# Top-k attention and two MLPs on one core: a planner writes the order of all five engines, and the first MLP's gate moves from VectorE to ScalarE and GpSimd

## The chip, the cores and the metric

One core of a Trainium2 chip runs the whole program. The metric is the device time of one execution in microseconds (us). A core has five engines, each with a queue of its own that it works through in order: TensorE (PE in the profile; its weight loads are shown as PEld), VectorE (DVE), ScalarE (ACT), GpSimd (POOL) and SyncE (SP), which here only issues DMAs.

## The reference

Everything is computed in float32 accuracy; the weights come as float64.

```
scores = q @ k.T / 8          # batch 4, heads 8, 576 x 576, head size 64
kth    = the 32nd largest score of each row
attn   = softmax of the scores >= kth, 0 elsewhere
x      = (attn @ v), heads side by side: 2304 x 512
h      = x @ w_in             # 512 x 2048
g      = h where h >= 1; 0 where h <= -1; (h + 1)^2 / 4 between
y      = g @ w_out            # 2048 x 512
h2     = max(y @ w_in2, 0)
out    = (h2 * h2) @ w_out2   # 2304 x 512
```

## The kernel before

**Tiles.** The 2304 tokens are 18 row tiles T of 128 rows. In attention a row tile has 8 slots, one for a head (two half heads where a tile straddles two batches), 144 slots in all. For each slot TensorE makes the scores (`scores`, L497 and L498), ScalarE copies them to SBUF (`scores_copy`, L502), and VectorE finds the 32 largest: four MAX8 (L514) with three MATCH_REPLACE8 between them (L516). ScalarE takes the exponential (`exp`, L528), with a bias that GpSimd makes (`exp_bias`, L523); VectorE multiplies it by the mask (`mask`, L532). ScalarE and GpSimd split the result into two float16 parts (`prob_hi` L544, `prob_lo` L548 and L549), a DMA transposes them (L554), and 14 matmuls multiply them with v (`attend`, L569) into one of 7 places of a PSUM bank, `acc`. The buffers `W` of the search and the exponential are a ring of three. `x_part` divides four slots by their sums and, after the second four, splits x and transposes it by DMA (L592) into `T_x`.

**The MLPs.** Each matrix is split into two float16 parts, so a product is three matmuls. A group n is a quarter of one layer of one row tile: 12 matmuls into a PSUM bank `h` (`mlp_in`, L710 to L712; two banks), the gate, the split of its result into `g`, a transpose by DMA to `gT` (`mlp_trans`, L746), and 12 matmuls into `o` (`mlp_out`, L757 to L759). There are 144 groups: 72 of the first MLP (m = 1) and 72 of the second (m = 2). They go in fours: four of the first MLP for tile T, then four of the second for tile T - 1. Between the two MLPs `y_finish` scales, splits and transposes y.

**The gate before.** With scaled constants, the first MLP's gate is min(square(relu(A1 h + B1)), relu(A2 h - G) + G). `mlp_act` makes the square in the buffer `r` (L721, L722) and the second relu in place of h in PSUM (L723), all on ScalarE; `mlp_gate` adds G and takes the minimum on VectorE (L733). `mlp_split` then takes a buffer `g` (a ring of two, `gbufs`), copies r into its first half as float16 on ScalarE (L740) and the remainder into its second half on GpSimd (L741). The second MLP's gate is a relu and a square on ScalarE (L725, L726).

**The weights** are loaded from float64 (64 chunks of 512 KB), put together by ScalarE, GpSimd and VectorE (`w_decode`, L181 to L183), measured by small matmuls (`w_norm`, L196), scaled and split (`w_scale`, `w_split`), all within the first 300 us or so.

**The order.** A plan by hand, `PLAN`, gives each piece of work a step; a slot is 8 steps. `at(u, fn, ...)` puts a call at step u, `chain` a list of calls at offsets from one, and `run_steps` calls them step by step; `early_fns` does the same for the search. The group with index n is at step 8 (12 + n), so a tile's first MLP comes some 12 slots after the slots of its index. VectorE and SP run in just the order of these calls (`MANUAL`, from step -6 on). The order of TensorE, ScalarE and GpSimd from there on is made by the framework, which simulates a timeline of the program while it is built.

Of the kernel before, what the change touches and what calls it, by code (L numbers as in the profile page):

```python
# [7 lines left out]
F16 = mybir.dt.float16  # L8
F32 = mybir.dt.float32
I32 = mybir.dt.int32  # L10
U16 = mybir.dt.uint16
BF16 = mybir.dt.bfloat16
AF = mybir.ActivationFunctionType
ALU = mybir.AluOpType
AX = mybir.AxisListType

P = 128
# [15 lines left out]


PLAN = dict(
    kch=(0, 0, 0, 1), vch=(0, 0, 1), scale=(0, 1, 2, 3, 4, 5), dch=(0, 1, 3), qch=(0, 0, 3, 4), k0=(-5, -4, -2),
    d0=(-8, -6, -4, -2), l0=(-9, -6), n0=(0, 1, 0, 1, 2, 3), q01=-5, v0l=-2, v0n=(5, 7, 9, 11), v0s=14, vn=60, vnd=7,
    vnl=18, vs=241, meet=248, mc1=252, m2c0=121, m2c1=265, v0=(21, 25, 29, 33, 37, 41, 45, 49), kv1=(254, 10, 289, 6),
# [13 lines left out]
    dsa_i2=(0, 2, 4, 6, 8, 10, 12, 14), dsa_o2=(0, 2, 4, 6, 8, 10, 12, 14), u0=-6,  # L52
    prio=(3, 0, 0, 2, 2, 3, 4, 5, 5, 6, 1, 7), gbufs=2, g_tr=18,
)
MANUAL = {mybir.EngineType.DVE, mybir.EngineType.SP}


@with_exitstack
def tile_topk_attention_mlp_mlp(
# [9 lines left out]
    out: bass.AP,  # L69
):  # L70
    nc = tc.nc
    PE, ACT, DVE, POOL, SP = nc.tensor, nc.scalar, nc.vector, nc.gpsimd, nc.sync

    cpool = ctx.enter_context(tc.tile_pool(name="cpool", bufs=1))
    pool = ctx.enter_context(tc.tile_pool(name="pool", bufs=2))
    small = ctx.enter_context(tc.tile_pool(name="small", bufs=2))
    ps_s = ctx.enter_context(tc.tile_pool(name="ps_s", bufs=1, space=bass.MemoryType.PSUM))
    ps_a = ctx.enter_context(tc.tile_pool(name="ps_a", bufs=1, space=bass.MemoryType.PSUM))
    ps_j = ctx.enter_context(tc.tile_pool(name="ps_j", bufs=1, space=bass.MemoryType.PSUM))
    ps_h = ctx.enter_context(tc.tile_pool(name="ps_h", bufs=2, space=bass.MemoryType.PSUM))  # L80
    ps_o = ctx.enter_context(tc.tile_pool(name="ps_o", bufs=2, space=bass.MemoryType.PSUM))

    def ctile(name, n=1):
        return cpool.tile([P, n], F32, tag=name, name=name)
# [130 lines left out]
    def w_split(name, c):  # L215
# [3 lines left out]
        if name in DIAG_AT:  # L219
# [106 lines left out]
    def k_prep(b, i):  # L326
        hl = lambda: ld["khl", b, i]

        on_dve = 4 * b + i in PLAN["dk"]

# [30 lines left out]
    def v_prep(b, h):  # L361
        on_dve = 8 * b + h in PLAN["dv"]

        def scale():
            t = ld["v", b, h]
            if not on_dve:
                POOL.tensor_scalar(t, t, sv[:, b : b + 1], 1.0, op0=ALU.mult, op1=ALU.mult)
            vs = pool.tile([P, 2, 5, D1], F16, tag="vst", name=f"vst_{b}_{h}", bufs=PLAN["vbufs"])
            POOL.memset(vs[:, 0, :, D : D + 1], 1.0)
            POOL.memset(vs[:, 1, :, D : D + 1], 0.0)  # L370
            vst[b, h] = vs

# [12 lines left out]

        return [scale, split_hi, split_lo]
# [4 lines left out]
    def tile_parts(T, j):  # L391

        if T in (4, 13):
            b = (0 if T == 4 else 2) + j // 4
            s0 = 512 if j < 4 else 0
            jj = j % 4
            return [(0, 64, b, 2 * jj, s0), (64, 64, b, 2 * jj + 1, s0)]
        if T < 4:
            b, s0 = 0, T * P
        elif T < 9:  # L400
            b, s0 = 1, 64 + (T - 5) * P
        elif T < 13:
# [21 lines left out]
    def q_scale(T):  # L424
# [268 lines left out]
    NGROUP = 8 * NTILE + 4  # L693
# [3 lines left out]
    def group(n):  # L697
        return group_[n]

    hps, gs, ops_, rt = {}, {}, {}, {}  # L700
# [11 lines left out]
        PE.matmul(h, src[:, 1, fb, :], w_hi(w, c, 0, 512), start=False, stop=(fb == 3))  # L712


    def mlp_act(n):
        m, T, j = group(n)
        r = pool.tile([P, 512], F32, tag="r", name=f"r_{n}", bufs=2)
        rt[n] = r
        h = hps[n].rearrange("p a b -> p (a b)")
        if m == 1:  # L720
            ACT.activation(r, h, AF.Relu, bias=B1[:, column(T)], scale=A1[:, column(T)])  # L721
            ACT.activation(r, r, AF.Square)  # L722
            ACT.activation(h, h, AF.Relu, bias=NG[:, column(T)], scale=A2[:, column(T)])  # L723
        else:
            ACT.activation(r, h, AF.Relu, scale=C2)  # L725
            ACT.activation(r, r, AF.Square)  # L726

    def mlp_gate(n):
        m, T, j = group(n)
        r = rt[n]  # L730
        if m == 1:
            h = hps[n].rearrange("p a b -> p (a b)")
            DVE.scalar_tensor_tensor(r, h, G[:, column(T)], r, op0=ALU.add, op1=ALU.min)  # L733
        del hps[n]

    def mlp_split(n):
        m, T, j = group(n)
        r = rt.pop(n)
        g = pool.tile([P, 2, 512], F16, tag="g", name=f"g_{n}", bufs=PLAN["gbufs"])
        ACT.activation(g[:, 0], r, AF.Copy)  # L740
        POOL.tensor_tensor(g[:, 1], r, g[:, 0], op=ALU.subtract)  # L741
        gs[n] = g

    def mlp_trans(n):
        t = pool.tile([P, 2, 4, P], F16, tag="gT", name=f"gT_{n}", bufs=2)
# [60 lines left out]
    ev = {}  # L806
# [9 lines left out]
    def at(u, fn, *args):  # L816
        ev.setdefault(u, []).append((fn, args))

    def chain(u, offsets, make, *args):
        def start():  # L820
            steps = make(*args)
            assert len(steps) == len(offsets), (make, len(steps))
            for o, step in zip(offsets, steps):
                if o:
                    at(u + o, step)
                else:
                    step()

        at(u, start)

    def k_chain(b, i, u):
        if b:
            at(u - PLAN["klead"], k_load, b, i)
# [27 lines left out]
    for c in range(2, 6):  # L861
        chain(PLAN["d0"][c - 2], PLAN["dch"], w_decode, "i1", c)
# [37 lines left out]
    dec = {n: PLAN["dec_" + n].__getitem__ for n in W}  # L900
# [24 lines left out]
    N0 = PLAN["N0"]  # L925
    order = [(1, 0, j) for j in range(4)] + ([(2, 0, j) for j in range(4)] if PLAN["early"] else [None] * 4)
# [49 lines left out]

    def run_steps(u0, u1):
        for u in range(u0, u1):
            fns = ev.pop(u, [])
            pre = [f for f in fns if f[0] in (scores, exp, exp_bias)]  # L980
            for fn, args in pre:
                if fn is not exp_bias:
                    fn(*args)
            early_fns(u)
            for fn, args in pre:
                if fn is exp_bias:
                    fn(*args)

            key = dict(zip((prob_hi, prob_lo, prob_trans, scores_copy, mlp_out, mlp_act, mlp_gate, mlp_split, mlp_trans, attend, attend, mlp_in), PLAN["prio"]))
            for fn, args in sorted((f for f in fns if f not in pre), key=lambda f: key.get(f[0], 9)):  # L990
                fn(*args)
            while u in ev:
                for fn, args in ev.pop(u):
                    fn(*args)

    with tc.manual_schedule():
        run_steps(-9, PLAN["u0"])
    with tc.manual_schedule(engines=MANUAL):
        run_steps(PLAN["u0"], 8 * (N0 + NGROUP + 6))
    assert not ev, sorted(ev)  # L1000


# [28 lines left out]
```

## Time and profile before

| what | value |
|---|---|
| median of 3 runs | 1179.51 us (1178.97 to 1180.36) |
| time of the profiled execution | 1181.12 us |
| its span, first to last instruction | 1179.3 us |
| mean granted TensorE clock | 0.968 of full speed |
| busy: PE, DVE, ACT, POOL | 1007.4, 979.3, 852.9, 685.5 us |
| the same as shares of the span | 85%, 83%, 72%, 58% |
| instructions | 20481 |

The busy time of an engine is the time in which it executes something; of TensorE the ends are modelled and overlap the next start, so the distance between starts tells more. The profile also lists groups of like instructions by line, what an engine waited for (and which engine's work released it), and the instructions in order of time. The profiled execution took 1.6 us more than the median.

### The profile page before, as it was taken

The page shows a single profiled execution, that of the slowest core. Times are in us where ns is not written, and L with a number is a line of the kernel's source. Part 1 is how long each engine was busy: PE and PEld are TensorE (multiplying, and loading weights), DVE is VectorE, ACT ScalarE, POOL GpSimd, SP SyncE. Part 2 cuts the span into 40 slices and gives each one's busy share as a digit, 9 for nine tenths or more (in the row PEclk, how much of TensorE's full clock was granted, in tenths as well). Part 3 has the DMA queues.
Part 4 walks back from the last instruction along what each step waited for, and adds up shares of the span by engine and source line. Part 5 has one row for each costly group of instructions (what it writes and reads, how often), then busy time and mean ns, then how long its engine had stood idle before and what let it go on. Part 6 is the DMA issues. An engine that isn't in the chain of part 4 may idle for free.

```text
span 1179.3 us, 20481 instructions
## 1 busy us (share of the span) xinstructions
PE 1007.4 (85%) x6700; PEld 488.3 (41%) x6700; DVE 979.3 (83%) x2111; ACT 852.9 (72%) x1613; POOL 685.5 (58%) x1004
## 2 busy tenths in 40 slices
PE   2248775568899999999888999999999999999997
PEld 1123332223344444444434444444444444444443
DVE  5798957958998999999888999999899999997100
ACT  5659987687677677878676887878676877867532
POOL 4774548858665745455766665456766555554221
PEclk9999988678899999999999999999999999999999
DMA  9977767665496766866886776767877666756532
GB/s 244 362 202 209 197 175 180 136 121 95 85 183 136 125 121 109 148 132 122 140 148 117 141 121 111 146 124 146 161 134 122 123 124 115 127 99 123 80 60 58
DMA packets 463386, 165.20 MB, mean 140 GB/s; under 512 B 441776, under 2 KB 448944, under 8 KB 463280
## 3 DMA queue, kind: packets, MB, share of 16 engines
q1 hardware_dynamic: 463280, 163.90, 68.6%
q8 instruction: 52, 0.85, 0.3%
q14 instruction: 54, 0.44, 0.1%
HBM read 55.31 MB, written 4.72 MB: 51 GB/s over the span
## 4 chain that ended last, share of the span: by engine, by line
PE 25%; DVE 24%; DMA 19%; ACT 12%; POOL 11%; issue 7%; SPq 2%; POOLq 0%; ACTq 0%; DVEq 0%
DVE W L516 9%; DVE m L514 8%; PE h L710 4%; DMA gT<-g 4%; PE o L757 4%; DVE W L532 4%; PE h L711 4%; PE h L712 4%; PE o L758 3%; PE o L759 3%; DMA T_x<-hl_x 3%; POOL g L741 2%; POOL S L549 2%; DMA qT<-qhl 2%; DMA wall<-in_moe_w_out_dram 2%
## 5 line engine op out<-in xcount | busy, mean ns | idle before, releaser
L514 DVE MAX8 m<-W 128x8 f32<-128x576 f32 x432 | 312.5, 745 | 0.1
L757 PE MATMUL o<-wall,gT 128*128 128x512 f16 x576 | 222.1, 386 | 25.7 <-DMA gT<-g 25.3
L741 POOL TENSOR_TENSOR g<-r,g 128x512 f16<-128x512 f32 x144 | 172.6, 1199 | 108.4 <-ACT g L740 70.0
L758 PE MATMUL o<-wall,gT 128*128 128x512 f16 x576 | 221.4, 384 | 0.0
L759 PE MATMUL o<-wall,gT 128*128 128x512 f16 x576 | 221.2, 384 | 0.0
L516 DVE MATCH_REPLACE8 W<-m,W 128x576 f32<-128x576 f32 x288 | 213.6, 742 | 0.0
L549 POOL TENSOR_TENSOR S<-W,S 128x512 f16<-128x512 f32 x144 | 167.4, 1162 | 0.0
L528 ACT ACTIVATE W<-S,nb,esc 128x576 f32<-128x576 f32 x144 | 124.7, 866 | 15.8 <-DVE m L514 15.0
L532 DVE SCALAR_TENSOR_TENSOR W<-S,m,W 128x576 f32<-128x576 f32 x144 | 134.1, 931 | 1.0 <-ACT W L528 1.0
L548 POOL TENSOR_TENSOR S<-W,S 128x64 f16<-128x64 f32 x144 | 46.9, 326 | 149.6 <-ACT S L544 148.9
L544 ACT ACTIVATE S<-W 128x576 f16<-128x576 f32 x144 | 98.1, 681 | 49.0 <-DVE W L532 48.4
L569 PE MATMUL acc<-vst,pT 128*128 128x65 f16 (+1 forms) x2240 | 106.2, 197 | 28.6 <-DMA pT<-S 26.8
L569 PEld LDWEIGHTS <-pT 128*128 128x128 f16 (+1 forms) x2240 | 94.6, 102 | 81.1 <-DMA pT<-S 36.4
L710 PE MATMUL h<-wall,T_x 128*128 128x512 f16 x288 | 112.0, 389 | 12.4 <-DMA T_x<-hl_x 11.2
L502 ACT ACTIVATE S<-s 128x576 f32<-128x576 f32 x144 | 93.0, 646 | 40.5 <-DMA pT<-S 20.6
L497 PE MATMUL s<-kst,qT 128*128 128x512 f16 (+1 forms) x320 | 99.3, 406 | 26.7 <-ACT S L502 14.6
L710 PE MATMUL h<-wall,T_y 128*128 128x512 f16 x288 | 110.1, 382 | 3.9 <-DVE r L733 3.8
L711 PE MATMUL h<-wall,T_x 128*128 128x512 f16 x288 | 111.4, 387 | 0.0
L712 PE MATMUL h<-wall,T_x 128*128 128x512 f16 x288 | 111.0, 385 | 0.0
L712 PE MATMUL h<-wall,T_y 128*128 128x512 f16 x288 | 110.2, 382 | 0.0
L711 PE MATMUL h<-wall,T_y 128*128 128x512 f16 x288 | 110.1, 382 | 0.0
L514 DVE MAX8 m<-S 128x8 f32<-128x576 f32 x144 | 107.9, 749 | 2.4 <-ACT S L502 2.4
(167 smaller groups left out, 1875.3 us busy)
## 6 DMA issues: line engine op xcount, KB each, us to landing
wall<-in_moe_w_in_dram SPq DMA_DIRECT2D x32, 512.0 KB, 6.1
wall<-in_moe_w_out_dram SPq DMA_DIRECT2D x30, 512.0 KB, 5.1
out_dram<-ob SPq DMA_DIRECT2D x18, 256.0 KB, 2.1
l_q<-in_q_dram SPq DMA_DIRECT2D x16, 256.0 KB, 3.8
n_v<-in_v_dram SPq DMA_DIRECT2D x24, 144.0 KB, 3.0
n_k<-in_k_dram SPq DMA_DIRECT2D x12, 288.0 KB, 3.1
l_k<-in_k_dram SPq DMA_DIRECT2D x12, 288.0 KB, 3.3
pT<-S SPq DMA_TRANSPOSE x144, 3.4
```

What stands on the lines that cost most here:

```text
L514: ops.append(lambda src=src, mi=mi: DVE.max(mi, src))
L516: ops.append(lambda src=src, mi=mi: DVE.match_replace(w, mi, src, -3.0e38))
L532: DVE.scalar_tensor_tensor(d["e"], d["s"], d["m"][:, TOPK - 1 : TOPK], d["e"], op0=ALU.is_ge, op1=ALU.mult,)
L549: POOL.tensor_tensor(pc[:, S + 64 :], p[:, 0:512], pc[:, 0:512], op=ALU.subtract)
L569: PE.matmul(acc[r0 : r0 + rn, t % 7, :], pT[:, pc, r0 : r0 + rn], vs[:, part, c, :], start=(i == 0), stop=(i == len(terms) - 1),)
L710: PE.matmul(h, src[:, 0, fb, :], w_hi(w, c, 0, 512), start=(fb == 0), stop=False)
L711: PE.matmul(h, src[:, 0, fb, :], w_lo(w, c, 0, 512), start=False, stop=False)
L712: PE.matmul(h, src[:, 1, fb, :], w_hi(w, c, 0, 512), start=False, stop=(fb == 3))
L741: POOL.tensor_tensor(g[:, 1], r, g[:, 0], op=ALU.subtract)
L757: PE.matmul(o, g[:, 0, fb, :], w_hi(w, c, 0, 512), start=(c == 0), stop=False)
L758: PE.matmul(o, g[:, 0, fb, :], w_lo(w, c, 0, 512), start=False, stop=False)
L759: PE.matmul(o, g[:, 1, fb, :], w_hi(w, c, 0, 512), start=False, stop=(c == 15))
```

## The change

Three things change. First, every call is now noted in a book instead of being issued; the book lists what each operation reads and writes, prices it, and then plans the five engines together. In the plan an engine that is free takes, among the operations that are ready, the one with the lowest rank, which is its step and then its place in the program. All five engines are then given the order of that plan. An operation may be planned at most 12 MAX8 ahead of its place (`WINDOW`), a load or store no earlier than the MAX8 just before it. Buffers of a ring are given out in the plan as they come free. Second, `soon` subtracts steps from the rank of some work: 8 steps for the scores and their copy, the exponential and its split and transpose, and `attend`; 24 steps for `x_part`. Third, the first MLP's gate becomes min(square(relu(A1 h + B1)) , G) + relu(A2 h - G), where the minimum is taken ahead of the square, with RHO, whose square is G: a new GpSimd tensor_scalar on r, the same ScalarE work (the second relu now goes to SBUF, into the buffer g, which is therefore taken in `mlp_act`), and a GpSimd addition in place of VectorE's instruction.

```diff
+    soon=dict(s=8, att=8, a=8, x=24),
-MANUAL = {mybir.EngineType.DVE, mybir.EngineType.SP}
...
+    def note(self, engine, method, fn, args, kwargs):
...
+        op.load = method == "dma_start"
+        if op.load:
+            if self.beat:
+                deps.add(self.beat[-1])
+        elif len(self.beat) > WINDOW:
+            deps.add(self.beat[-WINDOW])
+        if engine == "DVE" and method == "max":
+            self.beat.append(op.n)
...
+        op.key = (self.step + self.shift, op.n)
...
+    def costs(self, engine, method, args, kwargs, outs, ins):
+        n = outs[0].elements() if outs else 0
+        if engine == "PE":
+            a = args[1].tile.dtype
+            c = max(n * (4 if a is F32 else 1) / 2370.0, 0.044)
+            return c, c + 0.2
+        if engine == "DVE":
+            if method in ("max", "match_replace"):
+                n = 576
+            c = 0.06 + n / 960 + (0.07 if method != "max" else 0)
+            return c, c + 0.09
+        if engine == "ACT":
+            c = 0.17 + n / 1400 + 0.1 * sum(isinstance(kwargs.get(k), View) for k in ("bias", "scale", "accum_out"))
+            return c, c + 0.12
+        if engine == "POOL":
+            c = 0.2 + n / 550 if method == "tensor_tensor" else 0.22 + n / 1100
+            return c, c + 0.06
...
+            t, e = best
+            while soon[e] and soon[e][0][0] <= t:
+                op = ops[heapq.heappop(soon[e])[1]]
+                heapq.heappush(now[e], (op.key, op.n))
+            op = ops[heapq.heappop(now[e])[1]]
+            op.start = t
...
+WINDOW = 12
...
     def mlp_act(n):
         m, T, j = group(n)
         r = pool.tile([P, 512], F32, tag="r", name=f"r_{n}", bufs=2)
         rt[n] = r
-        h = hps[n].rearrange("p a b -> p (a b)")
+        h = hps.pop(n).rearrange("p a b -> p (a b)")
+        gs[n] = g = pool.tile([P, 2, 512], F16, tag="g", name=f"g_{n}", bufs=PLAN["gbufs"])
         if m == 1:
+            u = g.rearrange("p a b -> p (a b)").bitcast(F32)
             ACT.activation(r, h, AF.Relu, bias=B1[:, column(T)], scale=A1[:, column(T)])
-            ACT.activation(r, r, AF.Square)
-            ACT.activation(h, h, AF.Relu, bias=NG[:, column(T)], scale=A2[:, column(T)])
+            ACT.activation(u, h, AF.Relu, bias=NG[:, column(T)], scale=A2[:, column(T)])
+            POOL.tensor_scalar(r, r, RHO[:, column(T)], 0.0, op0=ALU.min, op1=ALU.max)
         else:
             ACT.activation(r, h, AF.Relu, scale=C2)
-            ACT.activation(r, r, AF.Square)
+        ACT.activation(r, r, AF.Square)
 
     def mlp_gate(n):
         m, T, j = group(n)
-        r = rt[n]
         if m == 1:
-            h = hps[n].rearrange("p a b -> p (a b)")
-            DVE.scalar_tensor_tensor(r, h, G[:, column(T)], r, op0=ALU.add, op1=ALU.min)
-        del hps[n]
+            POOL.tensor_tensor(rt[n], rt[n], gs[n].rearrange("p a b -> p (a b)").bitcast(F32), op=ALU.add)
 
     def mlp_split(n):
-        m, T, j = group(n)
-        r = rt.pop(n)
-        g = pool.tile([P, 2, 512], F16, tag="g", name=f"g_{n}", bufs=PLAN["gbufs"])
+        r, g = rt.pop(n), gs[n]
         ACT.activation(g[:, 0], r, AF.Copy)
         POOL.tensor_tensor(g[:, 1], r, g[:, 0], op=ALU.subtract)
-        gs[n] = g
...
+    def urgent(fn, made):
+        soon = SOON.get(KIND.get(fn, ""), 0)
+        if not soon:
+            return made
+
+        def call(*args):
+            book.shift, before = -soon, book.shift
+            made(*args)
+            book.shift = before
+
+        return call
...
-    with tc.manual_schedule():
-        run_steps(-9, PLAN["u0"])
-    with tc.manual_schedule(engines=MANUAL):
-        run_steps(PLAN["u0"], 8 * (N0 + NGROUP + 6))
-    assert not ev, sorted(ev)
+    run_steps(-9, 8 * (N0 + NGROUP + 6))
+    assert not ev, sorted(ev)
     with tc.manual_schedule():
+        book.emit(book.order())
```

## Rows read from the trace of the kernel before

**Rows 1.** Stretches of the span: busy us of each engine, its instructions, clock, DMA share.

```profile
0.00:420.00 420.00, 289.72 (x1933) 140.74 (x1934) 342.67 (x760) 310.27 (x609) 274.71 (x393) 0.92 0.72 174
420.00:1080.00 660.00, 626.41 (x4312) 306.11 (x4311) 625.37 (x1330) 499.71 (x934) 384.17 (x582) 0.99 0.71 129
```

**Rows 2.** The same stretches, line L532 (the mask, one a slot) alone.

```profile
420.00:1080.00 660.00, 91.93 (x99) 0.99 0.71 129
```

**Rows 3.** The same stretches, line L740 (the copy into g, one a group) alone.

```profile
420.00:1080.00 660.00, 60.90 (x98) 0.99 0.71 129
```

**Rows 4.** TensorE in order of time around 960 us: start, duration, instruction.

```profile
959.79 0.38 PE L710 MATMUL h<-wall,T_x 128*128 128x512 f16 x1
...
962.38 0.38 PE L757 MATMUL o<-wall,gT 128*128 128x512 f16 x1
...
965.62 0.38 PE L497 MATMUL s<-kst,qT 128*128 128x512 f16 x1
...
966.11 0.38 PE L569 MATMUL acc<-vst,pT 128*128 128x65 f16 x7
966.33 0.38 PE L757 MATMUL o<-wall,gT 128*128 128x512 f16 x1
```

**Rows 5.** The stretches of rows 1, line L733 (VectorE's gate) alone.

```profile
0.00:420.00 420.00, 11.81 (x16) 0.92 0.72 174
420.00:1080.00 660.00, 37.46 (x51) 0.99 0.71 129
```

**Rows 6.** What VectorE waited for from 0 to 420 us: total, times, longest.

```profile
DVE r L733 <- ACT r L722: 20.6, 3, 11.6
```

**Rows 7.** What VectorE waited for from 420 to 1080 us.

```profile
DVE W L516 <- POOL S L549: 9.3, 11, 2.5
...
DVE r L733 <- ACT r L722: 3.8, 5, 1.4
```

**Rows 8.** Groups of instructions, shapes apart: busy us, mean ns of one, idle before.

```profile
L741 POOL TENSOR_TENSOR g<-r,g 128x512 f16<-128x512 f32 x144 | 172.6, 1199 | 108.4 <-ACT g L740 70.0 <-issue 28.2 <-POOL S L549 2.9
...
L723 ACT ACTIVATE h<-h,NG,A 128x512 f32<-128x512 f32 x72 | 53.4, 741 | 0.0
L733 DVE SCALAR_TENSOR_TENSOR r<-h,G,r 128x512 f32<-128x512 f32 x72 | 53.0, 736 | 44.0 <-ACT r L722 43.5
...
L722 ACT ACTIVATE r<-r 128x512 f32<-128x512 f32 x72 | 45.1, 627 | 0.0
...
L434 POOL TENSOR_SCALAR l_q<-l_q,sq 128x512 f32<-128x512 f32 x18 | 13.6, 756 | 8.9 <-DVE sq L94 8.5
```

**Rows 9.** Line L532: shortest, median and longest duration in ns, first and last start.

```profile
L532 DVE SCALAR_TENSOR_TENSOR W<-S,m,W x144: 799/810/1660, 39.6 to 1084.5; 128x576 f32<-128x576 f32 x144
```

**Rows 10.** All engines in order of time: one group of the first MLP.

```profile
960.64 0.78 ACT L721 ACTIVATE r<-h,B,A 128x512 f32<-128x512 f32 x1 [0.78 <-PE h L712]
...
964.46 0.72 DVE L733 SCALAR_TENSOR_TENSOR r<-h,G,r 128x512 f32<-128x512 f32 x1
...
965.37 0.62 ACT L740 ACTIVATE g<-r 128x512 f16<-128x512 f32 x1
...
966.06 1.16 POOL L741 TENSOR_TENSOR g<-r,g 128x512 f16<-128x512 f32 x1 [0.17 <-ACT g L740]
...
967.50 1.27 SPq L746 DMA_TRANSPOSE gT<-g  x1
```

**Rows 11.** The DMAs into gT: us from issue to landing, shortest, median, longest.

```profile
DMA to landing us min/median/max: 3.0/3.1/5.4
```

**Rows 12.** 30 us with TensorE's clock lowered (columns as in rows 1).

```profile
210.00:240.00 30.00, 14.61 (x104) 7.71 (x104) 29.02 (x65) 22.04 (x49) 24.91 (x34) 0.65 0.58 130
```

**Rows 13.** VectorE in order of time: the last mask.

```profile
1084.47 1.16 DVE L532 SCALAR_TENSOR_TENSOR W<-S,m,W 128x576 f32<-128x576 f32 x1 [0.35 <-ACT W L528]
```

**Rows 14.** ScalarE in order of time: first and last of the 16 copies into g after it.

```profile
1086.91 0.63 ACT L740 ACTIVATE g<-r 128x512 f16<-128x512 f32 x1
...
1167.42 0.63 ACT L740 ACTIVATE g<-r 128x512 f16<-128x512 f32 x1
```

More of the change, by code (lines that the diff above doesn't have):

```diff
@@ L54, with __init__, __getitem__, _by @@
 )
-MANUAL = {mybir.EngineType.DVE, mybir.EngineType.SP}
+class View:
+    __slots__ = ("tile", "ap", "how")
+    def __init__(self, tile, ap, how=()):
+        self.tile, self.ap, self.how = tile, ap, how
+    def __getitem__(self, key):
+        return View(self.tile, self.ap[key], self.how + (("__getitem__", (key,), {}),))
+    def _by(self, name, *args, **kwargs):
+        return View(self.tile, getattr(self.ap, name)(*args, **kwargs), self.how + ((name, args, kwargs),))
+    def rearrange(self, *args, **kwargs):
+        return self._by("rearrange", *args, **kwargs)
+    def bitcast(self, dtype):
+        return self._by("bitcast", dtype)
+    def unsqueeze(self, axis):
+        return self._by("unsqueeze", axis)
+    def to_broadcast(self, shape):
+        return self._by("to_broadcast", shape)
+    def real(self):
+        at = self.tile.room()
+        for name, args, kwargs in self.how:
+            at = getattr(at, name)(*args, **kwargs)
+        return at
+    def cover(self):
+        size = SIZES[self.ap.dtype]
+        (pitch, parts), *free = self.ap.ap
+        p0, at = divmod(self.ap.offset, pitch)
+        free = sorted((s, n) for s, n in free if n > 1 and s)
+        run = 1
+        while free and free[0][0] == run:
+            run *= free.pop(0)[1]
+        last = at + run + sum(s * (n - 1) for s, n in free)
+        step = free[0][0] if len(free) == 1 else 0
+        return p0, p0 + parts, at * size, last * size, step * size, run * size
+    def elements(self):
+        n = 1
+        for _, m in self.ap.ap[1:]:
+            n *= m
+        return n
@@ new lines, with meet, __init__, room @@
+SIZES = {F16: 2, BF16: 2, U16: 2, F32: 4, I32: 4}
+def meet(a, b):
+    if a[1] <= b[0] or b[1] <= a[0] or a[3] <= b[2] or b[3] <= a[2]:
+        return False
+    step = a[4] or b[4]
+    if step and a[4] in (0, step) and b[4] in (0, step):
+        (x, nx), (y, ny) = ((c[2], c[5] if c[4] else c[3] - c[2]) for c in (a, b))
+        if nx < step and ny < step:
+            d = (y - x) % step
+            return d < nx or step - d < ny
+    return True
+class Room:
+    def __init__(self, ring, shape, dtype, name):
+        self.ring, self.shape, self.dtype, self.name = ring, shape, dtype, name
+        self.writes, self.reads, self.first, self.left, self.end, self.at = [], [], None, 0, 0.0, None
+    def room(self):
+        if self.at is None:
+            pool, kwargs = self.ring.pool, self.ring.kwargs
+            self.at = pool.tile(self.shape, self.dtype, name=self.name, **kwargs)
+        return self.at
@@ L58, in tile_topk_attention_mlp_mlp, with _bacc_ @@
+WINDOW = 12
+def _bacc_():
+    import concourse.bacc
+    return concourse.bacc
 @with_exitstack
@@ L71, in tile_topk_attention_mlp_mlp, with rings @@
     nc = tc.nc
[L72 to L81, printed above, removed]
+    book = Book(nc)
+    PE, ACT, DVE, POOL, SP = (
+        book.engine(n, e)
+        for n, e in (("PE", nc.tensor), ("ACT", nc.scalar), ("DVE", nc.vector), ("POOL", nc.gpsimd), ("SP", nc.sync))
+    )
+    def rings(name, bufs, **space):
+        return book.pool(ctx.enter_context(tc.tile_pool(name=name, bufs=bufs, **space)), bufs)
+    psum = dict(space=bass.MemoryType.PSUM)
+    cpool, pool, small = rings("cpool", 1), rings("pool", 2), rings("small", 2)
+    ps_s, ps_a, ps_j, ps_h, ps_o = (
+        rings(n, m, **psum) for n, m in (("ps_s", 1), ("ps_a", 1), ("ps_j", 1), ("ps_h", 2), ("ps_o", 2))
+    )
     def ctile(name, n=1):
@@ L817, in at @@
         ev.setdefault(u, []).append((fn, args))
+    SOON = PLAN["soon"]
+    KIND = {x_part: "x", mlp_in: "in", mlp_act: "act", mlp_gate: "act", mlp_split: "act", mlp_trans: "act", mlp_out: "out",
+            y_finish: "y", o_finish: "y", w_decode: "dec", w_norm: "dec", w_scale: "split", w_split: "split", norm: "n",
+            norm_load: "n", k_prep: "kv", v_prep: "kv", k_load: "kv", v_load: "kv", exp: "a", exp_bias: "a",
+            prob_hi: "a", prob_lo: "a", prob_trans: "a", attend: "att", scores: "s", scores_copy: "s", q_scale: "q", q_prep: "q"}
+    def urgent(fn, made):
[7 more added lines that the diff above has]
+        return call
     def chain(u, offsets, make, *args):
         def start():
-            steps = make(*args)
+            steps = [urgent(make, step) for step in make(*args)]
             assert len(steps) == len(offsets), (make, len(steps))
@@ L978, in run_steps @@
         for u in range(u0, u1):
+            book.step = u
             fns = ev.pop(u, [])
@@ L982, in run_steps @@
                 if fn is not exp_bias:
-                    fn(*args)
+                    urgent(fn, fn)(*args)
             early_fns(u)
@@ L986, in run_steps @@
                 if fn is exp_bias:
-                    fn(*args)
+                    urgent(fn, fn)(*args)
             key = dict(zip((prob_hi, prob_lo, prob_trans, scores_copy, mlp_out, mlp_act, mlp_gate, mlp_split, mlp_trans, attend, attend, mlp_in), PLAN["prio"]))
             for fn, args in sorted((f for f in fns if f not in pre), key=lambda f: key.get(f[0], 9)):
-                fn(*args)
+                urgent(fn, fn)(*args)
             while u in ev:
```

147 lines of the change are left out of this document (added).

## The prediction

> **What bounds the kernel now.** I read the stretches first, because shares of the whole span mix stages [rows 1]. From 420 to 1080 us VectorE is busy 625.4 of 660 us, 95%; TensorE shows 626.4, but its ends are modelled, so I count starts. Twelve matmuls of a group start from 959.79 to 962.38, 0.216 us apart; the four score matmuls take 0.49 us to the next start, seven of a slot's 14 `attend` matmuls 0.22 us [rows 4]. A slot costs TensorE 0.93 us, a group 24 x 0.216 = 5.18 us. The stretch holds 99 masks [rows 2] and 98 groups [rows 3], so TensorE needs 92 + 508 = 600 us of 660, 91%. The two engines run nearly level at one slot and one group per 6.67 us, VectorE ahead. Before 420 us neither is full: VectorE idles 77.3 us, and its longest single cause is the gate, which in the hand-written order waits for ScalarE's square 20.6 us in three places [rows 1, 6]. Behind each of those waits stand the next slot's MAX8 and the weights' decoding. At the end attention is over: the last mask ends at 1085.6 [rows 13], 16 groups still pass their copy into g [rows 14], and 93.7 us of matmuls follow, 5.18 us a group. So the time is VectorE's road to the last mask plus a tail of TensorE's.
>
> **The gate leaves VectorE.** Gone from 420 to 1080 us: 51 instructions, 37.5 us [rows 5], and 3.8 us of waiting for them [rows 7]. VectorE then needs 625.4 - 37.5 = 588 us there. ScalarE keeps its three instructions, so it costs nothing; the second relu writes SBUF instead of PSUM, priced as before at 0.74 us [rows 8]. GpSimd gets a tensor_scalar, nearest row 0.76 us (L434, same shape and type), and an addition, nearest row 1.20 us (L741, but float16 out): 1.96 us for each of 72 groups, 141 us [rows 8]. Their cover is GpSimd's idle time, 660 - 384 = 276 us in the stretch [rows 1], of which 51 x 1.96 = 100 us go: 58% busy becomes 77% of a stretch of 631 us. If that cover fails, VectorE's search is late next: its MATCH_REPLACE8 already waits 9.3 us for GpSimd to be done with an old W [rows 7]. Twice that would be 9 us more.
>
> **The two engines' common port.** The mask takes 0.81 us at the median, 1.66 at most [rows 9], 0.93 in the mean of the stretch [rows 2]: 0.12 us of it is excess, beside a GpSimd 58% busy. At 77% I put it at 0.16, so 99 masks cost 4 us more, and VectorE needs 592 us, still under TensorE's 600: nothing in the sum. The Trainium skill, page "SBUF — State Buffer", section "Who interferes with whom", speaks against the change here: a VectorE instruction with two SBUF inputs and a GpSimd instruction that reads SBUF exclude each other, and the later one is blocked until the other has ended. By that an average mask would lose half a GpSimd instruction times GpSimd's busy share, an estimate of 0.35 us now and 0.46 then, 11 us in the stretch, VectorE would stand level with TensorE, and the sum would be some 5 us later, 1130. The longest mask agrees with a full block, the median doesn't.
>
> **The planned order, 420 to 1080 us.** The floor is TensorE's 600 us. VectorE today fills 95% of its time; I give TensorE the same, 600 / 0.95 = 631, so **-29 us**. Ends: -60 (the floor) and 0 (today's pace stays, the freed time turns into waiting). I take the middle because the two loads, 600 and 592, lie so near each other that each will wait for the other.
>
> **The planned order, 0 to 420 us.** The gate's 20.6 us of waiting vanish, and of its 16 instructions' 11.8 us [rows 5] I count half, since VectorE has idle time to lose there: **-27 us**. Ends: -89 (all 77.3 us of idleness and the 11.8 filled) and +23. The loss end is the clock: TensorE's granted clock means 0.92 in this stretch [rows 1], 0.65 from 210 to 240 us, between its levels of 1.2 and 2.4 GHz, where it was busy 14.6 of 30 us [rows 12]. The planner prices every matmul at the full clock, and 8% of 289.7 us is 23. I stay near the middle, at the one wait that surely goes; weights and their decoding are late next.
>
> **Advance in rank.** x_part and its 18 transposes go ahead by 24 steps, the slots' ScalarE, GpSimd, TensorE and SP work by 8. They move past pT, gT and loads in SP's queue, an issue costing 1.27 us [rows 10], and past g's remainders on GpSimd. An issue moved ahead delays others by its own length and frees it later: 18 x 1.27 = 23 us of queue over the whole span, hidden because SP only issues. I cost it at 0, ends -10 and +23. The search's calls on VectorE don't pass through `urgent`, so their rank is unchanged.
>
> **The tail.** A planned step may be at most 12 MAX8, three slots, ahead, so a backlog of the same kind is left at the last mask. I take 0; ends -11 (16 groups at 5.18 are 83 us, against 93.7) and +5 (four last first-MLP groups whose chain grows by 1.96 - 0.74 = 1.2 us each, without other matmuls to cover it).
>
> **Sum.** 1181.1 (the profiled execution) - 29 - 27 = 1125; its like among the runs, at the median's distance of -1.6, would be 1123.5, and I keep **1125**.
>
> **Rivals.** *Slower: the ring of two g buffers.* A g is now taken at the second relu, not at the copy. Today it is held from 965.37 to the issue at 967.50 plus 3.1 us of transfer [rows 10, 11], 5.2 us. Afterwards: 0.76 + 0.63 + 1.20 + 0.62 + 1.20 on ScalarE and GpSimd and 3.1 of transfer, 7.5 us, plus six hand-overs. In today's group they cost 0.44 us each: 6.86 us from the first relu to the issue, of which 4.65 is work on the path, over five hand-overs [rows 8, 10]. That makes 10.2 us, or 5.1 us a group with two buffers, under the 6.4 us a slot and a group would then take. The ring decides from 12.8 us of holding on, 0.9 us a hand-over, twice today's. For it: in four first-MLP groups in a row GpSimd has 3.9 us a slot plus 1.96, 5.8 of 6.4, 91% busy, so what queues there waits. At 1.3 us a hand-over the hold is 15.3 us, 7.65 a group, 1.25 us too much for each of 72: +90, **1215**. Against it: the plan counts the ring and can put second-MLP groups between. *No gain: an order that is too tight.* The planner prices the mask at 0.06 + 0.60 + 0.07 = 0.73 us, the trace at 0.93 [rows 2]; in a fixed order 0.2 x 99 = 20 us of lateness can reach TensorE each time, and the early part may gain nothing: 1181 - 29 + 20 = 1172, and with GpSimd's W wait doubled, 1181; centre **1176**. *Better: the early stretch fills.* With 60 us instead of 27 early, and 45 instead of 29 later, **1076**. That the change doesn't do what it says is no case here beyond the unadvanced search: the gate's removal doesn't hang on ranks.
>
> **Chances and range.** Forecast (1085 to 1165) 0.60; better (under 1085) 0.06; too tight (1165 to 1190) 0.12, of which 0.05 is a gain, 0.05 no change, 0.02 a loss; the ring (over 1190) 0.22. A difference under 0.2% (2.4 us) can't be told from none here. So faster 0.71, same 0.05, slower 0.24. The range runs from 1085 to 1200: it leaves out the better case and two thirds of the ring's. The forecast's own range is 1085 to 1165.
>
> **What would show it.** Right: the gate's line gone from VectorE, masks per 60 us in the middle up from 9.0 to 9.4, the last mask near 1030, a tail still near 94 us, GpSimd busy near 825 us. The early part is right if VectorE's idle time before 420 us falls by some 20 us or more. Wrong: TensorE waiting for gT or `h` in first-MLP groups while ScalarE's second relu waits for a transpose that has not read g (the ring); a mask whose mean is over 1.1 us (the port); VectorE's MATCH_REPLACE8 waiting for GpSimd's remainder far beyond 20 us in all; TensorE's clock lower for longer than before.

## The result and the profile after

The changed kernel takes **1162.16 us** (median; 1160.56 to 1163.93) beside 1179.24 us for the kernel before: a ratio of 0.9866, with a 95% interval of 0.9847 to 0.9885. It is 1.3% faster, where 4.6% was forecast: 37 us over the forecast of 1125, inside the range of 1085 to 1200. Its profiled execution has a span of 1158.8 us, 20.5 us under the 1179.3 of before, so the two traces can be set against each other (the medians lie 17.1 us apart; the traced execution was the fastest of its four).

All instructions now come out of the book and so bear one line, L339 (L341 where a run's file is two lines longer); one tells them apart by tiles. First the page's busy times after, share of the span and instructions:

```profile
PE 1000.6 (86%) x6700; PEld 483.2 (42%) x6700; DVE 985.1 (85%) x2039; ACT 855.3 (74%) x1613; POOL 833.6 (72%) x1148
```

VectorE has 72 instructions fewer (2039 for 2111), those of the gate, which were 53.0 us of busy time [rows 8], and yet it is busy for 985.1 us where it was 979.3. GpSimd has 144 instructions more and is busy for 833.6 us (forecast: 825). The stretches of the kernel after, with the columns of [rows 1], cut shortly before its last mask:

```profile
0.00:420.00 420.00, 304.80 (x2073) 148.12 (x2074) 375.61 (x794) 329.39 (x644) 329.31 (x446) 0.93 0.77 182
420.00:1050.00 630.00, 594.75 (x4116) 289.12 (x4115) 602.46 (x1229) 477.48 (x890) 463.06 (x659) 1.00 0.69 129
```

In the middle VectorE reads 96% of the stretch (95% before [rows 1]) and holds 95 masks and 95 copies into g in 630 us: 6.63 us for a slot and a group, where it was 6.67. Nothing was gained there. To see where the 20.5 us came from I use the 40th of the 144 masks, well behind the weights, and the last one. In order of time on VectorE, before and then after:

```profile
397.33 1.13 DVE L532 SCALAR_TENSOR_TENSOR W<-S,m,W 128x576 f32<-128x576 f32 x1
```

```profile
363.92 0.81 DVE L339 SCALAR_TENSOR_TENSOR W<-S,m,W 128x576 f32<-128x576 f32 x1
...
1054.18 0.82 DVE L339 SCALAR_TENSOR_TENSOR W<-S,m,W 128x576 f32<-128x576 f32 x1 [0.99 <-ACT W L339]
```

With the last mask of before at 1084.47 [rows 13]: the start of the 40th comes 33.4 us earlier, the 104 slots from there to the last take 690.3 us for 687.1 (**+3.2**), and from the last mask to the end it is 104.6 for 94.8 us (**+9.8**). Together -20.4.

**Where VectorE's 53 us went.** Groups of the kernel after, shapes apart (busy us, mean ns | idle before); all second matmuls of the MLPs (`o`) are one group here:

```profile
L339 PE MATMUL o<-wall,gT 128*128 128x512 f16 x1728 | 425.2, 385 | 45.7 <-DMA gT<-g 42.9 <-POOL wall L339 1.3 <-DVE m L339 1.1
...
L339 DVE MAX8 m<-W 128x8 f32<-128x576 f32 x432 | 322.7, 753 | 5.0
L339 DVE SCALAR_TENSOR_TENSOR W<-S,m,W 128x576 f32<-128x576 f32 x144 | 145.7, 1012 | 4.6 <-ACT W L339 4.5
...
L339 POOL TENSOR_TENSOR r<-r,g 128x512 f32<-128x512 f32 x72 | 93.8, 1302 | 21.5 <-ACT r L339 21.3
...
L339 POOL TENSOR_SCALAR r<-r,RHO 128x512 f32<-128x512 f32 x72 | 51.2, 711 | 20.6 <-ACT r L339 20.3
```

and before, the same MAX8 and the first of the three lines of second matmuls, the only one with waits for gT:

```profile
L757 PE MATMUL o<-wall,gT 128*128 128x512 f16 x576 | 222.1, 386 | 25.7 <-DMA gT<-g 25.3
L514 DVE MAX8 m<-W 128x8 f32<-128x576 f32 x432 | 312.5, 745 | 0.1
```

The mask's mean rose to 1012 ns (931 before, the median of 810 unchanged), 11.6 us in all. More lies between the instructions. VectorE in order of time, first the order by hand, then the planned one:

```profile
453.16 0.74 DVE L516 MATCH_REPLACE8 W<-m,W 128x576 f32<-128x576 f32 x1
453.82 0.75 DVE L514 MAX8 m<-S 128x8 f32<-128x576 f32 x1
```

```profile
920.99 0.74 DVE L339 MATCH_REPLACE8 W<-m,W 128x576 f32<-128x576 f32 x1
921.76 0.76 DVE L339 MAX8 m<-W 128x8 f32<-128x576 f32 x1
923.10 0.76 DVE L339 MAX8 m<-S 128x8 f32<-128x576 f32 x1 [0.57 <-ACT S L339]
923.96 0.09 DVE L339 MATCH_VALUE_LOAD W<-m,S 128x8 f32 x1
```

The order by hand runs two searches in turn: the next instruction belongs to the other slot and starts 0.66 us after the one before, ahead of its end. In the planned order the MAX8 at 921.76 works on what the MATCH_REPLACE8 just before it wrote and starts 0.77 us after it, behind its end; the MATCH_VALUE_LOAD at 923.96 comes 0.86 us after the MAX8 that it needs. Counted over the trace (an instruction of over 0.5 us whose successor starts 20 to 110 ns after its end, not ahead of it) there are 12 such pairs before and 329 after, at 0.12 us and more each some 42 us of VectorE's time. With the masks that is 54 us: about what the gate had used.

### The profile page after: what moved, and what is told of

Same layout as the page of the kernel before. It is cut to its first block, busy times and chain, and to the rows that moved or that the text cites. A ratio compares the mean times of both kernels' runs of the same rounds, so it can differ in the third digit from the quotient of the medians.

```text
span 1158.8 us, 20462 instructions
## 1 busy us (share of the span) xinstructions
PE 1000.6 (86%) x6700; PEld 483.2 (42%) x6700; DVE 985.1 (85%) x2039; ACT 855.3 (74%) x1613; POOL 833.6 (72%) x1148
## 4 chain that ended last, share of the span: by engine, by line
DVE 28%; POOL 24%; PE 18%; DMA 12%; issue 8%; ACT 8%; SPq 1%; POOLq 0%; DVEq 0%; ACTq 0%
DVE W L339 14%; DVE m L339 11%; PE o L339 8%; PE h L339 8%; POOL wall L339 6%; POOL S L339 5%; DMA gT<-g 4%; POOL g L339 4%; POOL r L339 3%; ACT S L339 2%; DMA qT<-qhl 1%; ACT r L339 1%; SPq L339 1%; DMA wall<-in_moe_w_in_dram 1%; PE s L339 1%
## 5 line engine op out<-in xcount | busy, mean ns | idle before, releaser
L339 PE MATMUL o<-wall,gT 128*128 128x512 f16 x1728 | 425.2, 385 | 45.7 <-DMA gT<-g 42.9
L339 DVE MAX8 m<-W 128x8 f32<-128x576 f32 x432 | 322.7, 753 | 5.0
L339 PEld LDWEIGHTS <-gT 128*128 128x128 f16 x1728 | 160.8, 99 | 248.6 <-DMA gT<-g 69.0
L339 POOL TENSOR_TENSOR S<-W,S 128x64 f16<-128x64 f32 (+1 forms) x288 | 213.7, 760 | 69.5 <-ACT S L339 68.6
L339 POOL TENSOR_TENSOR g<-r,g 128x512 f16<-128x512 f32 x144 | 174.3, 1211 | 85.8 <-ACT g L339 65.5
L339 DVE MATCH_REPLACE8 W<-m,W 128x576 f32<-128x576 f32 x288 | 213.5, 741 | 0.0
L339 PE MATMUL h<-wall,T_x 128*128 128x512 f16 x864 | 207.3, 383 | 0.0
L339 PE MATMUL h<-wall,T_y 128*128 128x512 f16 x864 | 205.6, 379 | 1.0 <-ACT r L339 1.0
L339 ACT ACTIVATE W<-S,nb,esc 128x576 f32<-128x576 f32 x144 | 124.3, 863 | 38.8 <-DVE m L339 33.1
L339 DVE SCALAR_TENSOR_TENSOR W<-S,m,W 128x576 f32<-128x576 f32 x144 | 145.7, 1012 | 4.6 <-ACT W L339 4.5
L339 ACT ACTIVATE S<-W 128x576 f16<-128x576 f32 x144 | 98.3, 682 | 58.7 <-DVE W L339 54.6
L339 DVE MAX8 m<-S 128x8 f32<-128x576 f32 x144 | 107.7, 748 | 18.7 <-ACT S L339 18.6
L339 PE MATMUL s<-kst,qT 128*128 128x512 f16 (+3 forms) x640 | 103.9, 298 | 22.0 <-ACT S L339 18.7
L339 PEld LDWEIGHTS <-T_x 128*128 128x128 f16 x864 | 81.8, 99 | 93.2 <-issue 5.0
L339 PEld LDWEIGHTS <-T_y 128*128 128x128 f16 x864 | 81.3, 98 | 94.1 <-issue 2.6
L339 PE MATMUL acc<-vst,pT 128*128 128x65 f16 (+1 forms) x2240 | 100.8, 196 | 19.1 <-DMA pT<-S 9.7
L339 POOL TENSOR_TENSOR r<-r,g 128x512 f32<-128x512 f32 x72 | 93.8, 1302 | 21.5 <-ACT r L339 21.3
L339 PEld LDWEIGHTS <-pT 128*128 128x128 f16 (+1 forms) x2240 | 86.3, 102 | 54.5 <-DMA pT<-S 20.3
L339 ACT ACTIVATE g<-r 128x512 f16<-128x512 f32 x144 | 90.0, 625 | 24.1 <-POOL r L339 22.9
L339 DVE MATCH_REPLACE8 W<-m,S 128x576 f32<-128x576 f32 x144 | 106.9, 742 | 0.0
L339 ACT ACTIVATE S<-s 128x576 f32<-128x576 f32 x144 | 92.1, 640 | 12.0 <-PE s L339 11.9
L339 ACT ACTIVATE r<-r 128x512 f32<-128x512 f32 x144 | 90.5, 629 | 13.4 <-POOL r L339 11.5
```

Source lines behind the costliest of these rows:

```text
L339: op.fn(*(real(a) for a in op.args), **{k: real(a) for k, a in op.kwargs.items()})
```

## The experiments

Two doubts to settle: does the gain come from the order or from the gate, and why did the steady stretch gain nothing? All runs, with medians in us and ratios to the kernel before (95% interval):

| run | kernel | us | ratio |
|---|---|---|---|
| the change | planner, new gate | 1162.2 | 0.9866 [0.9847, 0.9885] |
| e1 | planner, old gate | 1150.7 | 0.9756 [0.9711, 0.9801] |
| e2 | order by hand, new gate | 1223.9 | 1.0374 [1.0334, 1.0413] |
| e10b | e2, MLP's later steps moved | 1211.7 | 1.0287 [1.0261, 1.0313] |
| e3 | the change, no advance | 1169.1 | 0.992 [0.9894, 0.9945] |
| e6 | the change, GpSimd's two left out | 1151.9 | 0.9774 [0.9748, 0.98] |
| e4 | the change, two prices | 1140.8 | 0.9674 [0.9637, 0.9712] |
| e7 | e4, scores 16 ahead | 1139.1 | 0.9664 [0.9633, 0.9695] |
| e8 | e4, GpSimd's prices | 1136.2 | 0.9637 [0.9613, 0.966] |
| e5 | old gate, two prices | 1129.5 | 0.9586 [0.9536, 0.9635] |
| e13 | e5, g taken early | 1130.3 | 0.9594 [0.9565, 0.9622] |
| e9 | e5, idle work on GpSimd | 1130.6 | 0.9593 [0.9573, 0.9612] |
| e14 | e5, longer chain | 1140.8 | 0.9688 [0.9659, 0.9717] |
| e11 | e5, scores 16 ahead | 1128.4 | 0.9586 [0.9555, 0.9617] |
| e12 | e5, GpSimd's prices, scores 24 ahead | **1126.7** | 0.9556 [0.9534, 0.9578] |

And the three parts of the span, from the starts of the 40th and the last mask in each trace:

| kernel | 40th mask | 40th to last | last to end |
|---|---|---|---|
| before | 397.3 | 687.1 | 94.8 |
| the change | 363.9 | 690.3 | 104.6 |
| e1 | 357.2 | 688.6 | 106.0 |
| e2 | 407.1 | 717.1 | 98.4 |
| e4 | 371.0 | 668.6 | 102.5 |
| e5 | 360.5 | 670.0 | 97.3 |
| e14 | 364.9 | 673.1 | 99.9 |
| e12 | 357.7 | 670.4 | 99.0 |

### One half of the change each: e1, e2, e10b

e1 is the changed kernel with `mlp_act`, `mlp_gate` and `mlp_split` of before; e2 is the kernel before with the three new ones; e10b is e2 with its later steps moved.

```diff
@@ e1, mlp_gate alone (e2 is the reverse, in the order by hand) @@
-            POOL.tensor_tensor(rt[n], rt[n], gs[n].rearrange("p a b -> p (a b)").bitcast(F32), op=ALU.add)
+            DVE.scalar_tensor_tensor(r, h, G[:, column(T)], r, op0=ALU.add, op1=ALU.min)
@@ e10b, on top of e2 @@
-    ... g_out=(20, 22, 23, 26), ... g_tr=18,
+    ... g_out=(22, 24, 25, 27), ... g_tr=20,
```

> The changed kernel with the gate put back on VectorE (the 72 instructions of 0.74 us, g taken at the copy); order and advance as changed. Theory A (VectorE stays the bound; the freed 48 us were lost again to dependent neighbours in its new order and to masks blocked by GpSimd): VectorE gets 48 us more and loses some neighbours and blocked masks, so the time goes up by 10 to 40 us, to 1172 to 1200. Theory B (the longer gate chain over GpSimd and the g ring set the pace, VectorE's lateness only fills waiting time): the time is 1162 or lower, down to 1145.

> The kernel before with the new gate alone; VectorE and SP keep the hand-written order, the rest the framework's. Theory A: the hand order interleaves two searches, so nothing is lost to neighbours, and VectorE's 48 us come out for the most part: 1135 to 1155, better than the change. Theory B: the gate chain on GpSimd stalls TensorE, 1175 or more.

> The hand-ordered kernel with the new gate (1224), g's transpose set two steps later in the order of SP and the second matmuls one to two steps later. If SP's fixed order is what turned the longer gate chain into +44 us (it stands before a gT transpose whose g is late, and the slots' pT transposes stand behind it): 1195 to 1215. If the chain itself is, wherever the transpose stands: 1219 to 1229.

**Measured:** 1150.7, 1223.9 and 1211.7 us; theory B in the first two, the range of the SP theory in the third. The order alone brings some 29 us, and the gate's move costs: 11.5 us under the planner, 44 under the order by hand. The early gain is the order's too: with the gate still on VectorE the 40th mask starts at 357.2, earlier than in the change (363.9), and in e2 it is late, at 407.1. In e2 SP, which issues in a fixed order, waits longer for the remainder; before, and e2 (total, times, longest):

```profile
SPq L746 <- POOL g L741: 59.3, 33, 4.9
```

```profile
SPq L742 <- POOL g L738: 83.4, 27, 10.9
```

e10b gives the transposes and what follows two steps more and gets 12 of the 44 us back. The other 32 I have not followed up. A first form of it with the steps one later still (e10) gave no kernel and so no time.

### Why the gate's move costs: e6, e13, e9, e14

e6 leaves the cap and the addition out of the computation, with the rest of the change in place. The other three build on e5 (below), which has the gate on VectorE: e13 writes the second relu into g, taken early as in the change; e9 gives GpSimd two instructions in each of 56 groups on a buffer that nobody waits for; e14 puts two instructions of GpSimd that change nothing between the gate and the copy.

```diff
@@ e6 @@
-            POOL.tensor_scalar(r, r, RHO[:, column(T)], 0.0, op0=ALU.min, op1=ALU.max)
...
-            POOL.tensor_tensor(rt[n], rt[n], gs[n].rearrange("p a b -> p (a b)").bitcast(F32), op=ALU.add)
@@ e13, mlp_act @@
+        gs[n] = g = pool.tile([P, 2, 512], F16, tag="g", name=f"g_{n}", bufs=PLAN["gbufs"])
...
+            u = g.rearrange("p a b -> p (a b)").bitcast(F32)
...
-            ACT.activation(h, h, AF.Relu, bias=NG[:, column(T)], scale=A2[:, column(T)])
+            ACT.activation(u, h, AF.Relu, bias=NG[:, column(T)], scale=A2[:, column(T)])
@@ e9, mlp_gate @@
+        if m == 1 and n >= 28:
+            spare = wall[:, 64, :]
+            POOL.tensor_scalar(spare, spare, 1.0, 0.0, op0=ALU.min, op1=ALU.max)
+            POOL.tensor_tensor(spare, spare, spare, op=ALU.mult)
@@ e14, mlp_gate @@
+        if m == 1:
+            POOL.tensor_scalar(r, r, 3.0e38, 0.0, op0=ALU.min, op1=ALU.max)
+            POOL.tensor_scalar(r, r, 3.0e38, 0.0, op0=ALU.min, op1=ALU.max)
```

> The changed kernel without GpSimd's two gate instructions (the cap and the addition are left out of what is computed; ScalarE's three stay), planned anew at the old prices with some 390 dependent neighbours. If GpSimd's 147 us of added work are what holds the change back (blocked masks, longer way from h to gT): 1140 to 1150. If the neighbours on VectorE alone are: 1160 or more.

> The run with the gate on VectorE and the trace's prices (1129.5), with g taken at the second relu, which writes into it, and VectorE's gate reading it from there: the buffer is held as early as in the change, and no GpSimd work is added. If the ring of two g is the cost: 1136 to 1142. If it is the chain over GpSimd: 1129 within 4 us.

> The run with the gate back on VectorE and the trace's prices (1129.5), with GpSimd made to do for 56 of the 72 first-MLP groups a cap and a product of the gate's size on a spare buffer, priced in the plan, that nobody waits for: some 110 us of GpSimd work with no chain behind it. If the mere load (the common port, other GpSimd work later) is what the moved gate costs: 1136 to 1142. If it is the longer way from h to gT: 1129 within 4 us.

> The same run with two GpSimd caps of 128x512 (0.7 us each, no effect on the values) put between VectorE's gate and the copy into g, so that the way from h to gT is longer by 1.4 us and a hand-over, as it is in the change by about as much, with 101 us more of GpSimd work. If the length of that way is the cost: 1135 to 1143. If not: 1129 within 4 us, as with the idle work.

**Measured:** e6 1151.9, between its two ranges and as e1: the two instructions carry the whole cost, and the rest of the gate's rewriting none that shows. It shows one thing more. In e6 neither VectorE nor GpSimd has a gate, and it is no faster than e1: under this plan the 53 us taken from VectorE bring nothing even when they cost nothing elsewhere. e13 lies 0.7 us over e5, within the intervals: an early g costs nothing there, where it is held 9.0 us from the second relu to the landing of gT (10.5 in the change). And e14, where g is taken late, pays as much as the change. e9 and e14 put the same load on GpSimd. The page's busy times of e9, then e14 (e5: POOL 687.8):

```profile
PE 999.8 (89%) x6700; PEld 486.1 (43%) x6700; DVE 987.9 (87%) x2111; ACT 851.8 (75%) x1613; POOL 783.3 (69%) x1116
```

```profile
PE 999.8 (88%) x6700; PEld 484.7 (43%) x6700; DVE 989.8 (87%) x2111; ACT 848.6 (75%) x1613; POOL 789.1 (69%) x1148
```

Beside the chain those some 100 us cost 1.0 us in time, within the intervals; in it, 11.3. e14 lies 10.2 us over e9, clear of both intervals. **In the order of e5 it is the length of the way from h to gT that costs, not GpSimd's load behind the 40th mask.** From the first relu's start to the remainder's end, a mean over the first MLP's groups between 420 and 1000 us, it is 6.65 us in e1 and 8.06 in the change, 7.06 in e5 and 9.45 in e14, which so lengthens it by more than the change does. The length compares within one order only: in the kernel before it is 8.74.

For the change itself this is not shown. e9's added work starts at 379.6 us, behind its 40th mask (361.7), while the change loses 6.7 of its 7.0 us against e1's trace ahead of that mask. There another wait has grown: MATCH_REPLACE8 waits until GpSimd is done with an old W. VectorE from 0 to 420 us, e1 and then the change (total, times, longest):

```profile
DVE W L339 <- POOL S L339: 3.3, 3, 1.2
```

```profile
DVE W L339 <- POOL S L339: 13.4, 11, 2.5
```

That is GpSimd being late with a slot's split, so the load on GpSimd's queue is a rival for the early part. A run with idle work in the first 16 first-MLP groups would test it; there is none.

### Why the steady stretch gained nothing: e3, e4, e5, e7

The planner's price for a small matmul is at least 0.044 us; `attend`'s start 0.031 us apart (seven in 0.22 us [rows 4]). Over 2240 of them the plan holds 29 us of TensorE that don't exist. And the mask is priced at 0.73 us where the trace has 0.93. e4 mends both, e5 is e1 with both mended, e7 is e4 with the scores 16 steps ahead, e3 takes all advance away.

```diff
@@ e4 (e5: 0.15, with the old gate) @@
-            c = max(n * (4 if a is F32 else 1) / 2370.0, 0.044)
+            c = max(n * (4 if a is F32 else 1) / 2370.0, 0.031)
...
+            if method == "scalar_tensor_tensor" and n == S:
+                c += 0.2
@@ e7, on top of e4 @@
-    soon=dict(s=8, att=8, a=8, x=24),
+    soon=dict(s=16, att=8, a=8, x=24),
@@ e3, on top of the change @@
-    soon=dict(s=8, att=8, a=8, x=24),
+    soon=dict(),
```

> The changed kernel without any advance in rank. Theory A: the advance is a side matter, 1162 within 10 us either way, as many dependent neighbours on VectorE. Theory B expects the same. A third theory (C, the advance is what made the change faster): 1175 or more.

> The changed kernel with two of the planner's prices set to the trace: an attend matmul at 0.031 us instead of 0.044, a mask at 0.93 instead of 0.73. The plan then believes VectorE, not TensorE, to be full, and gives it fewer dependent neighbours (about 140 planned instead of 340). Theory A: 200 fewer neighbours of 0.12 us, 24 us less busy on VectorE, time 1140 to 1150. Theory B: within 5 us of 1162.

> Both at once: the gate back on VectorE and the planner's prices set to the trace (attend matmul 0.031 us, mask 0.88). Planned dependent neighbours on VectorE: 35, against 342 in the change. Theory A1 (the neighbours are what the change lost on VectorE, and GpSimd's gate costs some 12 us by itself whatever the order): the two gains add, 1162 - 21 - 12 = 1129, within 1122 to 1136. Theory A2 (with right prices VectorE is full, so taking the gate off it pays after all): 1145 or more, slower than the run with the prices alone (1141). Theory A3 (both runs took away the same neighbours): 1138 to 1145.

> The changed kernel with the two prices of the trace and 16 steps of advance for the scores and their copy instead of 8, so that more slots stand ready for VectorE: 93 planned dependent neighbours instead of the 141 of the run with the prices alone (1141). If neighbours set VectorE's road: 48 x 0.12 = 6 us less, 1135. If what is left is GpSimd's doing: 1141 within 4 us.

**Measured:** 1169.1, 1140.8, 1129.5 and 1139.1 us. The prices bring 21.4 us with the new gate and 21.1 with the old, most of it in the steady stretch (690.3 to 668.6; 688.6 to 670.0); prices and gate add up, as theory A1 had it. Two rows of e4, TensorE's second matmuls and the mask:

```profile
L341 PE MATMUL o<-wall,gT 128*128 128x512 f16 x1728 | 420.9, 386 | 14.8 <-DMA gT<-g 14.5
L341 DVE SCALAR_TENSOR_TENSOR W<-S,m,W 128x576 f32<-128x576 f32 x144 | 156.8, 1089 | 7.7 <-ACT W L341 7.6
```

Its wait for gT falls from 42.9 to 14.5 us. That wait goes with the prices and not with the gate: 42.5 us in e1, 45.8 in e6, 17.6 in e5. As I read it, in a plan whose TensorE is slower than the real one the work ahead of gT may come late and be in time on paper; the real TensorE is there first and waits. The mask's mean rose again, to 1089 ns, and the kernel still won 21 us: slower masks did not undo the gain. The two prices were not run apart, so which of them brings how much is not shown.

Are the 329 pairs of dependent neighbours then the cause? e7 speaks against it: they fall from 141 in e4 to 87, VectorE's busy time from 974.4 to 961.4 us, and the time by 1.7 us, within the intervals. Its middle stretch is 12 us shorter (656.5), but two copies into g fewer fall in it, and the parts before and behind it are 3.4 and 5.4 us longer. e6 has 374 pairs and takes as long as e1 with 186. As I read it, the pairs come where VectorE has only one search at hand, and mostly fill time in which it would have waited. The advance is worth 6.9 us (e3).

### A faster version: e8, e11, e12

```diff
@@ e8, on top of e4; e12, on top of e5 and with s=24 (e11 is e5 with s=16) @@
-            c = 0.2 + n / 550 if method == "tensor_tensor" else 0.22 + n / 1100
+            c = 0.27 + n / 550 if method == "tensor_tensor" else 0.28 + n / 1100
```

> The run with the two prices, with GpSimd's prices raised to the trace as well (0.07 us more for a two-input instruction, 0.06 for the others). If GpSimd lags its plan and the fixed order then waits for it, knowing so helps: 1130 to 1137. If not: 1141 within 4 us, or slower, since its planned neighbours are 193.

> The gate on VectorE, the trace's two prices, and 16 steps of advance for the scores: 23 planned dependent neighbours instead of 35. By the neighbours 1128; the 8 steps more cost or give nothing else: 1129.5 within 4 us.

> The gate on VectorE, the trace's prices for attend, mask and GpSimd, and 24 steps of advance for the scores. GpSimd's prices gave 4.6 us with the gate on it; with 140 us less of its work there is less to gain: 1124 to 1130.

**Measured:** 1136.2, 1128.4 and 1126.7 us. e8 lies 4.6 us under e4. e12, the gate on VectorE and the prices nearer to the trace, is the fastest, 4.4% under the kernel before, though not clear of e11 and e5. Its middle stretch, with the columns of [rows 1]:

```profile
420.00:1020.00 600.00, 582.66 (x4051) 285.28 (x4049) 585.89 (x1251) 466.81 (x877) 366.50 (x556) 1.00 0.73 133
```

VectorE is busy for 98% of the stretch with the gate on it, TensorE shows 97%, and 26 pairs of dependent neighbours are left in the whole trace.

## Why the prediction was right and wrong

**The planned order, 420 to 1080 us: -29 us forecast, +3 measured.** This is the step that failed: "I give TensorE the same, 600 / 0.95 = 631". What came lies just outside the end that the text kept beside it, "0 (today's pace stays, the freed time turns into waiting)". In its place the runs show a plan made with wrong prices: of the 29 us of matmuls too many some 20 lie in this stretch (1498 `attend` matmuls of 0.013 us), and TensorE's waits for gT grew from 25.3 us in all before to 42.9. With the two prices mended together 40th to last mask gave -18.5 (e4) and -17.1 (e5). The 95% can be had: e12 holds 92 masks and 93 copies in 600 us, by the prediction's own count 567 us of TensorE, 94.6%. Both numbers for the small matmul were at hand, 0.044 in the diff and 0.031 in [rows 4], and were not set against each other.

**The gate leaves VectorE: forecast as the source of the gain, measured as a loss of 11.5 us.** VectorE's 588 us assumed the durations of the order by hand; a new order also decides what stands next to what, and the freed 53 us filled up again. Where the gate is gone altogether (e6) nothing is gained either: VectorE's gate was not what held the time. GpSimd's 141 us got a cover, "Their cover is GpSimd's idle time". Behind the 40th mask, and in the order of e5, it holds for load (e9) and not for links of a chain (e14); ahead of that mask, where the change lost most, which of the two fails is open. Their sizes were near: 1.30 us for the addition (forecast 1.20) and 0.71 for the cap (0.76).

**0 to 420 us: -27 forecast, -33 measured at the 40th mask, but for another reason.** The text took it from the gate's waits on VectorE, which would go with the gate. e1 keeps the gate there and has -40; VectorE waits 0.2 us for it before 420 us, where it was 20.6, because the order changed. The move gave 7 us back.

**The tail: 0 forecast, +10 measured.** The forecast's "a backlog of the same kind" was wrong, and the end of +5 too near. Counted in matmuls, behind the last mask stand 20 groups' second products for 18 before and 17 groups' first products for 15: two groups at 5.18 us. At the 40th mask the change is behind in the MLPs too (22.5 groups' first products for 26.0), so the search has run further ahead of them, and some of the early gain is paid back here. e1 has 106.0 us and e5 97.3, so with the old gate most of it goes with the prices; in e4, with the new gate, 102.5 us stay.

**Advance: 0 forecast, worth 6.9 us**, inside its ends of -10 and +23.

**The rivals.** The ring showed as no bound (e13), and its hold was sized well: 10.5 us from the second relu to the landing of gT, where 10.2 were forecast and 12.8 would have been needed. "An order that is too tight" (centre 1176) had the right mechanism, a planner with wrong prices, but only for the mask. The port's cost, 0.16 us a mask forecast, was 0.20 (1012 ns against the median of 810), and the time didn't hang on it. The Trainium skill, page "SBUF — State Buffer", section "Who interferes with whom", calls the port pair that the two engines share an exclusive lock, and the trace agrees; the prediction had read the median mask as a sign against it. GpSimd and VectorE in the change:

```profile
648.11 1.16 POOL L339 TENSOR_TENSOR g<-r,g 128x512 f16<-128x512 f32 x1
648.42 1.46 DVE L339 SCALAR_TENSOR_TENSOR W<-S,m,W 128x576 f32<-128x576 f32 x1
```

In the change 47 masks start while a GpSimd TENSOR_TENSOR of over 0.5 us has over 0.2 us left to run, and all 47 end 0.61 to 0.62 us after its end; before it is 37 of 37. The median mask is one that starts at another time. What was too high is the estimate of 0.46 us: it took GpSimd's busy share for the share of masks that are blocked, and that is some 47 of 144, with GpSimd 72% busy.

That e12 takes 1126.7 us, near the forecast of 1125, is chance: its three parts differ from before by -39.6, -16.7 and +4.2 us, and the gate is where it was.

**Left open.** Whether the chain or GpSimd's load costs the change its 6.7 us ahead of the 40th mask. By which single wait a longer chain costs 11 us in e14: the total of TensorE's waits for gT is the same in e1 and in the change (42.5 and 42.9), and lower in e14 than in e5 (12.9 and 17.6). In the change nearly all of the loss shows before the 40th mask (357.2 to 363.9), in e14 only 4.4 of the 10.1 us between the two spans (1127.8 and 1137.9). A third buffer for r was not tried.

## What to carry to other kernels

A planner's price list is a part of the kernel: set each price against the distance between starts in the trace before believing its order, since two wrong ones, by 0.013 us for a small matmul and 0.2 us for a mask, cost 21 us, more than the gate's move. Work moved to an idle engine has two prices, as load and as a link of a chain (1.0 and 11.3 us here): ask how much longer the chain becomes that another engine waits for at the end of it. And an engine's busy time is no measure of its need: VectorE did 72 instructions fewer and was busy for longer. Count the work done in the stretch.

## What the runs showed of the hardware

A VectorE instruction that needs the one just before it starts behind that one's end, 0.777 us after its start for a MAX8 on what MATCH_REPLACE8 wrote, where one of another search starts 0.659 us after it, ahead of its end; for MATCH_VALUE_LOAD behind the MAX8 of fresh scores it is 0.847. The Trainium skill, page "VectorE: DVE Perf Modes", section "The DRAIN you can't avoid", reports that a semaphore between successive VectorE copies cost nothing; here dependence on the neighbour cost 0.118 us, so the measurement decides for this search. GpSimd at 69% instead of 61% busy, with 100 us of instructions that nobody waited for, moved the time by 1.0 us only, though a mask that finds GpSimd in a TENSOR_TENSOR waits for its end (47 of 47 in the change): the mask's mean went from 949 ns in e5 to 963 in e9.
